# A fused attention and soft-MoE kernel rewritten: resident weights, longer q/k runs, two-bank score tiles, dispatch per batch, experts in column tiles, a hand-set order

## The chip, the core and the metric

The kernel runs on one core of a Trainium2 chip. The core has a matrix engine (TensorE, PE in the profile; its weight loads are listed apart as PEld), a vector engine (VectorE, DVE), a scalar engine (ScalarE, ACT), GpSimd (POOL) and SyncE (SP). They run side by side, each through its own list of instructions in order, and meet through semaphores. Transfers between memory and the core's buffer (SBUF) are queued by POOL or SP and carried out by 16 shared transfer engines. TensorE writes to a small accumulator memory (PSUM, eight banks of 512 float32 columns), from which VectorE and ScalarE read.

The metric is the time of one execution in microseconds, on the device. Where the profile gives a granted clock for TensorE, 1.00 stands for 2.4 GHz and 0.50 for 1.2 GHz.

## The reference, cut

Two stages follow each other. First attention with 4 batches, 8 heads, 768 positions and 64 columns per head: a head is either causal over the whole sequence or, by a flag, causal over the first 4 positions and a window of 64. Its output, 3072 tokens of 512 columns, goes through a soft mixture of 8 experts with 4 slots each.

```python
scores = scale * np.matmul(q, k.transpose(0, 1, 3, 2))
scores = np.where(mask[None], scores, -1e9)      # causal, or sinks and window, by is_retrieval[h]
a = np.exp(scores - scores.max(-1, keepdims=True))
a = a / (a.sum(-1, keepdims=True) + 1e-9)
x = np.matmul(a, v)                              # -> (3072, 512)

logits = x @ phi                                 # (3072, 32)
d = softmax(logits, axis=0)                      # over tokens
slot_input = (d.T @ x).reshape(8, 4, 512)
for e in range(8):
    slot_out[e] = np.maximum(slot_input[e] @ w1[e], 0.0) @ w2[e]   # 512 -> 1024 -> 512
c = softmax(logits, axis=1)                      # over slots
out = c @ slot_out.reshape(32, 512)
```

## The kernel before

Everything is computed in bf16 with float32 sums. The kernel is written as plain loops, and a scheduler orders the instructions of each engine by priority as buffers come free; so heads overlap.

**Setup.** POOL builds the masks, and queues the load of the eight flags (L159) ahead of the first q. VectorE makes a mask per head (L168 to L173).

**Attention** (`_attention`, a loop over 4 batches and 8 heads). For each pair of heads `_load_T2` loads q and k (L22, one transfer per head and tensor, in runs of 64 elements), transposes them on TensorE in six blocks of 128 x 128 that hold both heads (L26), and copies the result out of PSUM on VectorE (L29). v comes with one transfer per head (L50) into a tile with a column of ones; a second copy of it, v_far, is scaled by the head's flag (L56, L58) and serves key blocks more than one block away. For each of six key blocks j the scores of all later queries are computed with keys as the stationary operand (L69, 64 rows, at most 512 columns at once) into a tile of 768 float32 columns, of which there are two; ScalarE takes exp (L77), and VectorE multiplies the first 256 columns by the mask (L79). For each of six query blocks i, PV sums over j (L86, 21 matmuls of 65 columns a head), VectorE copies the sum (L90), and after all six takes the reciprocal of the ones' column (L92) and multiplies (L93) into x.

**Logits.** When attention is done, each of 24 token blocks is transposed in four pieces (L198, L199), multiplied by phi (L202), put through exp (L204) and transposed back (L206, L207). **Slots**: sums over tokens (L210 to L216), 24 matmuls of 512 columns (L223), a scaling (L225), four transposes (L228).

**Experts.** w1 and w2 of each expert, 1 MB each in bf16, are loaded by POOL (L240, L243) into rings of four buffers each. The instruction's place in POOL's list is behind all q, k and v loads. Per expert: 32 matmuls with a block of w1 as stationary operand and 4 columns (L250), relu (L256), 8 matmuls with 4 stationary columns and 512 moving columns of w2 (L259), a copy (L262) and a transfer to a scratch tensor in DRAM (L263); at the end one transfer brings all 32 rows back (L264).

**Output.** 24 matmuls of 512 columns (L270), a scaling on VectorE (L272) and a transfer by POOL that casts to float32 (L273).

## Time and profile before

| | |
|---|---|
| time, median of 3 runs (lowest to highest) | 361.65 us (361.61 to 361.93) |
| span of the profiled execution | 359.7 us |
| PE busy | 265.5 us, 74% |
| PE weight loads busy | 123.0 us, 34% |
| DVE busy | 178.2 us, 50% |
| ACT busy | 114.0 us, 32% |
| POOL busy | 113.3 us, 32% |
| moved by transfers | 32.91 MB, mean 91 GB/s |
| transfer packets, of them under 512 B | 92967, 77520 |

The profiled execution's own time is its span; the runs' median lies 1.95 us above it. The shares are averages over stages that differ: TensorE is busy nearly throughout attention and logits, and the transfer engines are busy nearly throughout the experts' stage, where the engines wait.

### The profile page before, as it was taken

How to read it: one execution, taken by the hardware profiler on the slowest of the kernel's cores; microseconds unless marked ns; L12 is line 12 of the kernel's file. 1: busy time of each engine (PE TensorE's matmuls, PEld its weight loads, DVE VectorE, ACT ScalarE, POOL GpSimd, SP SyncE). 2: the span in 40 equal slices, each digit the busy share in tenths (PEclk: the TensorE clock that was granted, in tenths of full speed). 3: DMA queues.
4: the chain of work that ended last, by engine and by line, in shares of the span. 5: the costliest groups of instructions: out<-in, count | busy, mean ns of one | idle time of the engine just before them, and what ended most of it. 6: DMA issues, size and time to landing. Idle time of an engine off the chain costs nothing.

```text
span 359.7 us, 4849 instructions
## 1 busy us (share of the span) xinstructions
PE 265.5 (74%) x1708; PEld 123.0 (34%) x1708; DVE 178.2 (50%) x725; ACT 114.0 (32%) x233; POOL 113.3 (32%) x165
## 2 busy tenths in 40 slices
PE   0048998999999999999989899996462445553661
PEld 0023444445454544545443444442221112220110
DVE  0096677676686867777576655554100000000684
ACT  1004564655646466465655211110010000000000
POOL 9395434526353453642010000006020100000463
PEclk9999999999999999999999999999876555556555
DMA  0799946959769597974230000009999999993698
GB/s 0 41 132 73 62 31 45 72 39 78 49 46 70 35 76 46 65 48 26 20 22 3 0 0 2 1 0 146 210 210 210 207 210 209 210 210 55 168 302 233
DMA packets 92967, 32.91 MB, mean 91 GB/s; under 512 B 77520, under 2 KB 85776, under 8 KB 92944
## 3 DMA queue, kind: packets, MB, share of 16 engines
q0 software_dynamic: 92832, 32.55, 74.9%
q8 instruction: 13, 0.21, 0.2%
q14 instruction: 10, 0.08, 0.1%
q1 hardware_dynamic: 112, 0.07, 0.1%
HBM read 52.53 MB, written 6.32 MB: 164 GB/s over the span
## 4 chain that ended last, share of the span: by engine, by line
PE 54%; DMA 26%; DVE 8%; POOL 5%; issue 3%; ACT 3%; POOLq 0%; DVEq 0%; SPq 0%; ACTq 0%
PE sc L69 23%; DMA w2t<-in_moe_w_dram 21%; PE pv L86 13%; PE tp L26 5%; PE tp L198 5%; PE lg L202 5%; DMA r_f__67<-in_is_retrieval_dram 4%; POOL out_dram L273 3%; ACT p_Ts L77 2%; PE sp L259 2%; DVE p_Ts L79 2%; DVE pvs L90 1%; DVE x_sb L93 1%; DVE dst L29 1%; DVE mask_j L168 1%
## 5 line engine op out<-in xcount | busy, mean ns | idle before, releaser
L77 ACT ACTIVATE p_Ts<-sc 128x768 bf16<-128x768 f32 (+2 forms) x192 | 100.3, 543 | 96.6 <-PE sc L69 91.1
L69 PE MATMUL sc<-dst 64*128 64x512 bf16 (+3 forms) x256 | 101.1, 465 | 3.8 <-ACT p_Ts L77 3.1
L86 PEld LDWEIGHTS <-p_Ts 128*128 128x128 bf16 x672 | 44.8, 127 | 51.4 <-issue 39.2
L79 DVE TENSOR_TENSOR p_Ts<-p_Ts,mask_j 128x256 bf16<-128x256 bf16 x192 | 50.2, 272 | 17.9 <-ACT p_Ts L77 15.3
L272 DVE TENSOR_SCALAR ofin<-op,rrow 128x512 bf16<-128x512 f32 x24 | 16.6, 746 | 81.9 <-PE op L270 81.3
L90 DVE COPY pvs<-pv 128x65 f32<-128x65 f32 x192 | 39.7, 222 | 33.2 <-PE pv L86 30.8
L86 PE MATMUL pv<-v_ext,p_Ts 128*128 128x65 bf16 x352 | 55.2, 244 | 1.2 <-DVE p_Ts L79 1.2
L26 PE MATMUL tp<-identity,raw 128*128 128x128 bf16 x192 | 31.5, 305 | 23.0 <-DMA raw<-in_q_dram 18.8
L259 PE MATMUL sp<-w2t,hT 128*4 128x512 bf16 x64 | 26.3, 585 | 25.6 <-DMA w2t<-in_moe_w_dram 25.6
L86 PE MATMUL pv<-v_far,p_Ts 128*128 128x65 bf16 x320 | 37.9, 243 | 3.9 <-DVE pvs L90 3.9
L22 POOL DMA_DIRECT2D raw<-in_q_dram x32 | 26.5, 834 | 35.2 <-PE pv L86 28.9
L69 PEld LDWEIGHTS <-dst 64*128 64x128 bf16 x256 | 25.4, 112 | 28.8 <-issue 14.6
L22 POOL DMA_DIRECT2D raw<-in_k_dram x32 | 26.5, 835 | 20.0 <-PE tp L26 19.6
L26 PEld LDWEIGHTS <-raw 128*128 128x128 bf16 x192 | 17.7, 131 | 35.7 <-DMA raw<-in_q_dram 22.8
L273 POOL DMA_DIRECT2D out_dram<-ofin x24 | 12.9, 536 | 50.5 <-DVE ofin L272 48.1
L240 POOL DMA_DIRECT2D w1t<-in_moe_w_dram x8 | 6.1, 767 | 71.5 <-ACT exp_lg_T L204 59.0
L50 POOL DMA_DIRECT2D v_ext<-in_v_dram x32 | 26.3, 826 | 1.8 <-issue 0.5
L199 DVE COPY xTc<-tp 128x128 bf16<-128x128 bf16 x96 | 19.5, 225 | 13.9 <-PE tp L198 12.8
L198 PE MATMUL tp<-identity,x_sb 128*128 128x128 bf16 x96 | 24.0, 282 | 1.1 <-DVE xTc L199 0.7
L202 PE MATMUL lg<-xTc,phi_sb 128*32 128x128 bf16 x96 | 23.3, 295 | 0.0
L262 ACT CAST sp_sb<-sp 4x512 bf16<-4x512 f32 x8 | 4.6, 575 | 54.9 <-PE sp L259 54.9
L259 PEld LDWEIGHTS <-hT 128*4 128x4 bf16 x64 | 7.1, 112 | 39.1 <-issue 35.2
(49 smaller groups left out, 173.5 us busy)
## 6 DMA issues: line engine op xcount, KB each, us to landing
w1t<-in_moe_w_dram POOLq DMA_DIRECT2D x8, 1024.0 KB, 34.3
w2t<-in_moe_w_dram POOLq DMA_DIRECT2D x8, 1024.0 KB, 33.5
out_dram<-ofin POOLq DMA_DIRECT2D x24, 256.0 KB, 2.3
raw<-in_q_dram POOLq DMA_DIRECT2D x32, 96.0 KB, 3.3
raw<-in_k_dram POOLq DMA_DIRECT2D x32, 96.0 KB, 3.4
v_ext<-in_v_dram POOLq DMA_DIRECT2D x32, 96.0 KB, 3.5
so_d<-sp_sb SPq DMA_DIRECT2D x8, 4.0 KB
phi_sb<-in_moe_phi_dram POOLq DMA_DIRECT2D x1, 32.0 KB, 2.9
```

What stands on the lines that cost most here:

```text
L22: nc.gpsimd.dma_start(raw[:, :, hh, :], src_ap[hh].rearrange("(so si) d -> si so d", si=P))
L26: nc.tensor.transpose(tp[:, blk * P : (blk + 1) * P], raw[:, blk, :, :].rearrange("p h d -> p (h d)"), identity)
L50: nc.gpsimd.dma_start(v_ext2[:, :, kk, :D], v[b, h + kk].rearrange("(so si) d -> si so d", si=P),)
L69: nc.tensor.matmul(sc[:, cs : cs + cl], k_T2[po : po + D, j * P : (j + 1) * P], q_T2[po : po + D, j * P + cs : j * P + cs + cl], start=Tru ...
L77: nc.scalar.activation(p_Ts[:, j, :sq_len], sc[:, :sq_len], ACT.Exp, scale=SCALE)
L79: nc.vector.tensor_mul(p_Ts[:, j, :dp], p_Ts[:, j, :dp], m[:, h, :dp])
L86: nc.tensor.matmul(pv, p_Ts[:, j, loc : loc + P], vv[:, j, :], start=(j == 0), stop=(j == i),)
L90: nc.vector.tensor_copy(pvs[:, i, :], pv)
L198: nc.tensor.transpose(tp, x_sb[:, nci, db * P : (db + 1) * P], identity)
L202: nc.tensor.matmul(lg, phi_sb[:, db, :], xTc[:, db, :], start=(db == 0), stop=(db == DB - 1))
L259: nc.tensor.matmul(sp, hT[:, fb, :], w2ts[e][:, fb, :], start=(fb == 0), stop=(fb == FB - 1))
L273: nc.gpsimd.dma_start(out[nci * P : (nci + 1) * P, :], ofin)
```

## The change

Nearly every line is new; what is computed stays. By parts:

- **Weights.** All of w1 and w2 has its own SBUF space (`w1s`, `w2s`). `w_load` queues one half of one matrix (0.52 MB in bf16, rows of 4 KB in SBUF); one is queued per pair of heads up to pair 12 and the remaining 19 at pair 13, all by POOL.
- **q and k.** One transfer per tensor and pair of heads, with six consecutive positions of 64 elements as one run per partition. The transposes then take 64 columns of one head each, 12 per tensor and pair, into rows 0 to 63 or 64 to 127 of the PSUM tile; the copy out restores the order. q is copied by VectorE, k by ScalarE.
- **Scores.** Six key blocks in three groups, (0, 4), (1, 3) and (5, 2), each in one tile of two banks (1024 columns); exp runs once per group, on 1024, 1024 and 640 columns, and the mask multiplies once per group.
- **PV** of a head stands one head behind its scores, in one PSUM tile for all six query blocks; the normalisation reads PSUM.
- **Logits, exp over tokens and dispatch** come once per batch, within attention, two to four heads after the batch has ended. phi is repeated four times over the columns, so that exp of logits fills 128 rows. The dispatch writes four groups of 32 rows, which are summed later.
- **Experts.** slot inputs are the stationary operand (32 columns), weights the moving one (512 columns); four experts write to four groups of 32 rows of one tile. A mask per expert (`emask`) keeps each one's four slots. No scratch tensor in DRAM.
- **Output.** Evictions alternate between ScalarE and VectorE into float32 tiles of three blocks; SP queues eight transfers.
- **Order.** `tc.manual_schedule()`: each engine runs its instructions as the code emits them.

The core of the diff, new lines:

```diff
+GROUPS = [[0, 4], [1, 3], [5, 2]]
+    def load_qk(self, n):
+            t = self.raw.tile([128, 2, 384], BF16, tag=tag, name=tag)
+            self.nc.gpsimd.dma_start(t, src[b, h:h + 2].rearrange("h (p s) d -> p h (s d)", s=6))
+    def transpose_qk(self, n, which):
+        for s in range(6):
+            for i in range(2):
+                self.nc.tensor.transpose(tp[64 * i:64 * (i + 1), s * 128:(s + 1) * 128],
+                                         src[:, i, s * 64:(s + 1) * 64], self.ident)
+    def qk(self, t, g):
+        sc = self.scp.tile([128, 1024], F32, tag="sc", name="sc")
+        for j in GROUPS[g]:
+            ...
+                nc.tensor.matmul(sc[:, o:o + w], kT[po:po + 64, j * 128:(j + 1) * 128],
+                                 qT[po:po + 64, q0:q0 + w], start=True, stop=True)
+        nc.scalar.activation(pT[:, GBASE[g]:GBASE[g] + GLEN[g]], sc[:, :GLEN[g]], ACT.Exp,
+                             scale=self.scale)
+    def logits(self, b):
+        for c0, cl in ((0, 512), (512, 256)):
+            for db in range(4):
+                nc.tensor.matmul(lg[:, c0:c0 + cl], self.phi4[:, db, :], self.xT[b][:, db, c0:c0 + cl],
+                                 start=(db == 0), stop=(db == 3))
+    def dispatch(self, b):
+        for i in range(6):
+            g = i % 4
+            nc.tensor.matmul(sp[32 * g:32 * (g + 1), :], self.elg[b][:, i, :], self.xb[b][:, i, :],
+                             start=(i < 4), stop=(i + 4 >= 6))
...
+    ctx.enter_context(tc.manual_schedule())
...
+        for t in range(NT + 1):
+            n = t // 2
+            if t % 2 == 0:
+                if t < NT:
+                    if n + 3 < NT // 2:
+                        at.load_qk(n + 3)
+                    if n + 2 < NT // 2:
+                        at.load_v(n + 2)
+                for _ in range(1 if n < 13 else 4 * NE):
+                    if wi < 4 * NE:
+                        w_load(wi)
+                        wi += 1
+            if t < NT:
+                at.qk(t, 0)
+                at.mask(t, 0)
+            if t >= 1:
+                at.pvmm(t - 1, 0)
+                at.pvmm(t - 1, 1)
+            if t < NT:
+                at.qk(t, 1)
+                at.mask(t, 1)
+            if t >= 1:
+                for i in (2, 3, 4):
+                    at.pvmm(t - 1, i)
+            if n + 1 < NT // 2 and t < NT:
+                at.transpose_qk(n + 1, "q" if t % 2 == 0 else "k")
+            if t < NT:
+                at.qk(t, 2)
+            if t >= 1:
+                at.pvmm(t - 1, 5)
+                at.norm(t - 1)
+            if t < NT:
+                at.mask(t, 2)
+            if t % 2 == 1 and t >= 3:
+                at.x_transpose((t - 3) // 2)
+            if t >= 8:
+                b, r = (t - 8) // 8, (t - 8) % 8
+                if r == 2:
+                    at.logits(b)
+                elif r == 3:
+                    at.exp_tokens(b)
+                elif r == 4:
+                    at.dispatch(b)
...
+            for c in range(2):
+                for do in range(4):
+                    for g in range(4):
+                        nc.tensor.matmul(hp[32 * g:32 * (g + 1), c, :], siT[:, do, :],
+                                         w1s[4 * e4 + g][:, do, c * 512:(c + 1) * 512],
+                                         start=(do == 0), stop=(do == 3))
```

How the new order stands on the engines, at three places. In each piece L-numbers are lines of the program in question.

TensorE within a head of attention. Before, the scheduler puts single transposes (`tp`, from `raw`), scores (`sc`) and PV (`pv`) between one another as they become ready:

```order
L69 LDWEIGHTS dst
L69 MATMUL sc<-dst 128x256
L69 LDWEIGHTS dst
L69 MATMUL sc<-dst 128x128
L26 LDWEIGHTS raw
L26 MATMUL tp<-identity,raw 128x128
...
L86 LDWEIGHTS p_Ts
L86 MATMUL pv<-v_ext_1752,p_Ts 128x65
L26 LDWEIGHTS raw
L26 MATMUL tp<-identity,raw 128x128
```

Now the same place, behind the PV matmuls of query block 4 and with the transposes of the next pair's q (`qr`) ahead of the last group of scores:

```order
L136 LDWEIGHTS pT
L136 MATMUL pv<-vb_134,pT 128x65
L73 LDWEIGHTS qr
L73 MATMUL tp<-ident,qr 64x128
...
L104 LDWEIGHTS kT
L104 MATMUL sc<-qT,kT 128x128
L104 LDWEIGHTS kT
L104 MATMUL sc<-qT,kT 128x384
```

The work of one kind now stands together (12 transposes in a row, then three scores), and each transpose writes 64 rows where it wrote 128.

TensorE in the experts. Before, an expert's w1 is the stationary operand and 4 columns move:

```order
L250 LDWEIGHTS w1t_3303
L250 MATMUL hp<-slot_in_T,w1t_3303 128x4
L250 LDWEIGHTS w1t_3307
L250 MATMUL hp<-slot_in_T,w1t_3307 128x4
```

Now the slots are stationary and 512 columns of w1 of four experts (`w_0` to `w_3`) move in turn, each into its own 32 rows of `hp`:

```order
L393 LDWEIGHTS siT
L393 MATMUL hp<-w_0_60,siT 32x512
L393 LDWEIGHTS siT
L393 MATMUL hp<-w_1_61,siT 32x512
L393 LDWEIGHTS siT
L393 MATMUL hp<-w_2_62,siT 32x512
L393 LDWEIGHTS siT
L393 MATMUL hp<-w_3_63,siT 32x512
```

256 matmuls of 4 columns and 64 of 512 have become 128 of 512, neighbours in different groups of rows.

POOL's list of transfers. Before, the first weights stand behind the last v load, and from the fifth expert on each load waits for a buffer:

```order
L48 MEMSET v_ext_2557 128x12
L50 DMA v_ext_2557<-in_v_dram 128x6x64 x2
L240 DMA w1t_3303<-in_moe_w_dram 128x4x1024
L243 DMA w2t_3305<-in_moe_w_dram 128x8x512
L240 DMA w1t_3307<-in_moe_w_dram 128x4x1024
```

Now one half stands behind each pair's q, k and v, and the rest behind the last v:

```order
L58 DMA qr<-in_q_dram 128x2x384
L58 DMA kr<-in_k_dram 128x2x384
L65 DMA vb_132<-in_v_dram 128x6x64 x2
L230 DMA w_6_66<-in_moe_w_dram 128x2048
L65 DMA vb_134<-in_v_dram 128x6x64 x2
L230 DMA w_6_66<-in_moe_w_dram 128x2048
L230 DMA w_7_67<-in_moe_w_dram 128x2048 x2
L235 DMA w_0_68<-in_moe_w_dram 128x2048 x2
L235 DMA w_1_69<-in_moe_w_dram 128x2048 x2
```

The weights have moved ahead of attention's end, and no load of them waits for a buffer.

## Rows read from the trace of the kernel before

**Rows 1.** Windows by stage: window, length, busy time per engine, clock, DMA share, GB/s.
```profile
core 0: us, PE busy (x) PEld busy (x) DVE busy (x) ACT busy (x) POOL busy (x), PEclk, DMA share, GB/s
25.30:200.00 174.70, 165.70 (x1103) 82.37 (x1102) 122.48 (x539) 100.28 (x192) 68.61 (x95) 1.00 0.74 48
200.00:242.40 42.40, 40.98 (x219) 18.42 (x216) 24.72 (x124) 6.41 (x24) 0.00 (x0) 1.00 0.00 1
242.40:256.20 13.80, 8.92 (x29) 3.37 (x29) 5.90 (x9) 0.00 (x0) 6.57 (x8) 1.00 0.98 162
256.20:331.20 75.00, 34.45 (x321) 14.55 (x320) 0.17 (x1) 6.04 (x16) 6.56 (x8) 0.57 1.10 195
...
334.40:359.70 25.30, 13.16 (x24) 2.55 (x24) 16.60 (x24) 0.00 (x0) 12.86 (x24) 0.50 0.90 249
```

**Rows 2.** The chain that ended last, by line, from the page.
```profile
PE sc L69 23%; DMA w2t<-in_moe_w_dram 21%; PE pv L86 13%; PE tp L26 5%; PE tp L198 5%; PE lg L202 5%; DMA r_f__67<-in_is_retrieval_dram 4%; POOL out_dram L273 3%; ACT p_Ts L77 2%; PE sp L259 2%; DVE p_Ts L79 2%; DVE pvs L90 1%; DVE x_sb L93 1%; DVE dst L29 1%; DVE mask_j L168 1%
```

**Rows 3.** Windows, four heads in the middle of attention.
```profile
103.89:125.44 21.55, 20.71 (x141) 10.52 (x142) 15.53 (x68) 12.51 (x24) 10.15 (x14) 1.00 0.88 57
```

**Rows 4.** Timeline of TensorE in attention: start us, us, engine line op, tiles.
```profile
158.20 0.61 PE L69 MATMUL sc<-dst 64*128 64x512 bf16 x1
158.74 0.34 PE L86 MATMUL pv<-v_far,p_Ts 128*128 128x65 bf16 x3
158.90 0.30 PE L86 MATMUL pv<-v_ext,p_Ts 128*128 128x65 bf16 x2
159.13 0.50 PE L69 MATMUL sc<-dst 64*128 64x384 bf16 x1
159.56 0.40 PE L86 MATMUL pv<-v_far,p_Ts 128*128 128x65 bf16 x4
```

**Rows 5.** Timeline of weight loads and matmuls around two rises of the clock.
```profile
250.87 0.15 PEld L223 LDWEIGHTS <-exp_lg 128*32 128x32 bf16 x1 [0.28 <-issue]
251.30 0.15 PEld L223 LDWEIGHTS <-exp_lg 128*32 128x32 bf16 x1 [0.28 <-issue]
251.66 1.82 PEld L223 LDWEIGHTS <-exp_lg 128*32 128x32 bf16 x9 [0.21 <-issue]
...
262.24 3.36 PE L259 MATMUL sp<-w2t,hT 128*4 128x512 bf16 x8
...
266.71 1.89 PE L259 MATMUL sp<-w2t,hT 128*4 128x512 bf16 x8 [0.74 <-DMA w2t<-in_moe_w_dram]
```

**Rows 6.** Windows, two stretches of the experts' stage.
```profile
265.00:275.00 10.00, 3.85 (x54) 2.01 (x53) 0.00 (x0) 1.44 (x4) 3.28 (x4) 0.84 1.18 209
275.00:285.00 10.00, 4.59 (x40) 1.86 (x40) 0.00 (x0) 0.77 (x2) 1.64 (x2) 0.50 1.18 209
```

**Rows 7.** Start: a piece of the chain, TensorE's first work, q's transfers from the page.
```profile
3.81 13.63 DMA r_f__67<-in_is_retrieval_dram
18.82 0.80 PE L26 MATMUL tp<-identity,raw 128*128 128x128 bf16 x6 [18.82 <-DMA raw<-in_q_dram]
raw<-in_q_dram POOLq DMA_DIRECT2D x32, 96.0 KB, 3.3
```

**Rows 8.** Groups by line and shape: busy us, mean ns, idle before.
```profile
L77 ACT ACTIVATE p_Ts<-sc 128x768 bf16<-128x768 f32 x32 | 26.0, 811 | 65.2 <-PE sc L69 61.3 <-DVE pvs L90 3.9
L77 ACT ACTIVATE p_Ts<-sc 128x128 bf16<-128x128 f32 x32 | 8.8, 276 | 4.3 <-PE sc L69 3.7
L79 DVE TENSOR_TENSOR p_Ts<-p_Ts,mask_j 128x256 bf16<-128x256 bf16 x160 | 44.4, 282 | 14.8 <-ACT p_Ts L77 12.6
L79 DVE TENSOR_TENSOR p_Ts<-p_Ts,mask_j 128x128 bf16<-128x128 bf16 x32 | 7.1, 222 | 3.1 <-ACT p_Ts L77 2.7
L29 DVE COPY dst<-tp 128x768 bf16<-128x768 bf16 x32 | 17.5, 548 | 1.1 <-PE tp L26 1.1
```

**Rows 9.** Output: an eviction's group, and windows of one stretch.
```profile
L272 DVE TENSOR_SCALAR ofin<-op,rrow 128x512 bf16<-128x512 f32 x24 | 16.6, 746 | 81.9 <-PE op L270 81.3 <-DMA out_dram<-ofin 0.6
340.00:343.00 3.00, 1.98 (x4) 0.38 (x4) 2.32 (x4) 0.00 (x0) 1.72 (x5) 0.50 1.11 309
```

More of the change, by code (lines that the diff above doesn't have):

```diff
@@ L9 @@
 from concourse._compat import with_exitstack
-from concourse.masks import make_identity
 F32 = mybir.dt.float32
@@ L266 @@
[L266 to L273 removed]
+    n_sink, window = int(n_sink), int(window)
@@ new lines, with w_load @@
+    ES = moe_phi.shape[1]
+    NE, DM, F = moe_w1.shape
+    SPE = ES // NE
+    ctx.enter_context(tc.manual_schedule())
+    singles = ctx.enter_context(tc.tile_pool(name="singles", bufs=1))
+    w1s = [singles.tile([P, 4, F], BF16, name=f"w1_{e}") for e in range(NE)]
+    w2s = [singles.tile([P, 8, DM], BF16, name=f"w2_{e}") for e in range(NE)]
+    def w_load(i):
+        if i < 2 * NE:
+            e, half = i // 2, i % 2
+            nc.gpsimd.dma_start(
+                w1s[e][:, 2 * half:2 * half + 2, :],
+                moe_w1[e].rearrange("(di do) f -> di do f", do=4)[:, 2 * half:2 * half + 2, :])
+        else:
+            e, half = (i - 2 * NE) // 2, i % 2
+            nc.gpsimd.dma_start(
+                w2s[e][:, 4 * half:4 * half + 4, :],
+                moe_w2[e].rearrange("(fi fo) d -> fi fo d", fo=8)[:, 4 * half:4 * half + 4, :])
@@ new lines @@
+    with tc.tile_pool(name="osb", bufs=4) as osb, \
+         tc.tile_pool(name="ops", bufs=6, space=PSUM) as ops:
+        for b in range(B):
+            er = expT[:, b, :].rearrange("p (t r) -> p r t", r=6)
+            ov = out[b * S:(b + 1) * S, :].rearrange("(p r) d -> p r d", r=6)
+            for half in range(2):
+                ot = osb.tile([P, 3, DM], F32, tag="ot", name="ot")
+                for r3 in range(3):
+                    r = 3 * half + r3
+                    op = ops.tile([P, DM], F32, tag="op", name="op")
+                    nc.tensor.matmul(op, er[:, r, :], slot_out, start=True, stop=True)
+                    if (6 * b + r) % 2:
+                        nc.scalar.activation(ot[:, r3, :], op, ACT.Copy, scale=rrow[:, b, r:r + 1])
+                    else:
+                        nc.vector.tensor_scalar_mul(ot[:, r3, :], op, rrow[:, b, r:r + 1])
+                nc.sync.dma_start(ov[:, 3 * half:3 * half + 3, :], ot)
```

474 lines of the change are left out of this document (262 added, 212 removed).

## The prediction

> **What bounds the kernel now.** I read the stages first [rows 1]. Each ends where its last instruction's result is wanted, and no two overlap: a start of 25.3 us before the first score matmul, 174.7 us of attention, 42.4 us of logits, 13.8 us of slots, 75.0 us of experts, 3.2 us of hand-over and 25.3 us of output. Then the chain by line [rows 2]: scores (L69) and PV (L86) hold 36% of the span, and the largest single item is the transfer of w2, 21%. So two things bound it: TensorE while attention and logits run, and the transfer queue while the experts run.
>
> In attention, four heads take 21.55 us and TensorE is busy 20.71 of them, against 15.53 for VectorE and 12.51 for ScalarE [rows 3]. A head costs 5.39 us. The column for the clock reads 1.00 there, yet the starts of matmuls say otherwise: a score of 384 columns is followed by PV 0.43 us later, one of 512 columns 0.54 us later [rows 4]. So 128 columns cost 0.11 us, 1.2 per ns, the lower of the two levels (1.2 and 2.4 GHz). The slot matmuls show the same spacing, 0.43 us, up to 251.3, and from 251.66 on nine weight loads in 1.82 us, about 0.21 us each [rows 5]; so the column's 1.00 before that moment doesn't describe the engine, and all of attention ran at 1.2 GHz. Before the rise TensorE had run the slots' full-height 512-column matmuls (L223) back to back; the experts' eight from 262.24 on are the same kind of run, and the next eight, at 266.71, go in 1.89 us [rows 5]. Some 230 us of attention and logits, TensorE busy nearly throughout, did not raise it.
>
> In the experts stage the transfers move 209 GB/s into SBUF, with the queue's share at 1.18, for 10 us on end [rows 6]; 16.8 MB of weights by that rate is 80 us, and TensorE is busy 34 of the stage's 75 us [rows 1]. The weights are not asked for before the logits end, so all of it lies in the open.
>
> **The change part by part.** I sum the new program at 1.2 GHz, stage by stage, in the profiled execution's own time; the median of the runs is 1.95 us above the span of 359.7.
>
> *Start.* Before, the first q load is queued behind the flags' load of 13.63 us, and the first transpose starts at 18.82 [rows 7]. Now the flags go through SP's queue and q is first in POOL's. Bounds for its landing: the median 3.3 us [rows 7], or again 13 us. I take 3.3, since the row with 13 us has the flag load ahead of it. With four short memsets ahead, k behind it, two sets of transposes and two copies of 0.55 us [rows 8], the first score matmul comes at 8 us (7 to 16).
>
> *A head in attention.* Scores: 2688 columns as before, 2.24 us at 0.43 per 512. PV: 21 matmuls, 0.054 apart (three between 158.74 and 158.90), 1.13 us. Transposes: they double from 6 to 12 per head, since each takes one head's 64 columns; two neighbours write the two halves of the array's columns. If they run together, six times 128 columns at 1.2 per ns, 0.64 us; one by one 1.27. Changes between 64-row scores and full-height work cost: 512 columns are 0.43 us by the spacing of the slot matmuls [rows 5], and 0.54 where PV follows; the second of the two PV from 158.90, so at 158.95, is followed by scores after 0.18 instead of 0.05 [rows 4]; about 0.12 each. The new order has seven per head, 0.84 us; before there are 302 over 32 heads by the program's order, 9.4 each, 1.13 us. What is left of the 5.39 after 2.24, 1.13, 0.64 and 1.13 is 0.25 us of waits; I take 0.30. Sum: 5.15 us a head (5.78 with single transposes), 165 us for 32.
>
> *ScalarE and VectorE* I cost at nothing under that cover. Exp of 1024, 1024 and 640 columns by the line through 768 and 128 columns [rows 8] is 1.03 + 1.03 + 0.70; half a copy of k, 0.41 at most, and logits' share 0.1 give 3.26 us a head. VectorE: three masks of 512, 512 and 384 columns, 0.40 + 0.40 + 0.34, normalising 384 columns under the 0.55 of a copy of 768, a reciprocal under the 0.22 of a mask of 128, half of two copies 0.55, far values of 260 columns 0.28: 2.74 us. Both are below 5.15. If TensorE doubles its speed, ScalarE's 3.26 is the bound; that is the second rival.
>
> *Logits and slots* move into attention: transposes of x, 15 × 0.64 = 9.6 us; per batch 3072 columns of logits 2.56, six transposes 0.64, six one-column sums 0.3 at PV's spacing, dispatch of six 512-column matmuls in four column tiles 0.85 (two rounds), two changes 0.24: 4.6 us, three times 13.8. The fourth is in the tail. So attention is 165 + 9.6 + 13.8 = 188 us. The long full-height runs may raise the clock for a while; between 265 and 275 it was up for part of the time (0.84) and from 275 on no more [rows 6], so a rise lasts some 7 us and saves 3. For two of three batches I take 6 us off: 182.
>
> *Tail to the experts.* Last PV 1.1, normalising 0.8, transposes of x and copy 1.2, logits 2.56, exp 0.8, transposes and copy 0.9, dispatch 0.85, add and scaling 0.75 each like an eviction [rows 9], slot transposes and copy 0.6: 10.3, with hand-overs 11 us. It replaces 42.4 + 13.8.
>
> *Experts.* 128 matmuls of 512 columns, four at a time in column tiles: 32 rounds. The first 16 at 0.43, 6.8 us; relu 0.6; 16 transposes 1.7 and a copy 0.9; the second 16 between 3.5 us at 0.21 and 6.8, I take 5.2; copies 0.4. 16 us instead of 75, and the round trip through DRAM (3.2) is gone.
>
> The Trainium skill, page "TensorE: Matmul & The Clock Gate", Part 3, says that a weight load overlaps a running matmul only where the two use different rows of the array; column tiles share all rows, so by it each of the four would wait for its neighbour. The trace does not agree: loads of the same rows lie inside the 0.43 us of the running 512-column matmul and cost nothing [rows 5]. By the page the sum would be that of the first rival, by the row it stays.
>
> *Weights.* 32 halves of 0.52 MB. POOL queues one per pair of heads, and from pair 13 on the last 19 without any wait; the wait ahead of them is for pair 11's buffer, some 24 heads in, at 8 + 24 × 5.47 + 9 = 148 us (5.47 with the share of x's transposes, 9 for two batches' logits and slots). 19 × 0.52 MB at 209 GB/s is 48 us, so they land by 196; the second half of the experts, which wants them, starts at 8 + 182 + 11 + 8 = 209. Attention hides them, with 13 us to spare. Ahead of that POOL has two q/k loads fewer per pair. Twelve loads keep the queue at 0.88 for 21.55 us [rows 3]; a pair now brings four loads and 2.5 us of weights in 10.9 us.
>
> *Output.* 6.3 MB at the 309 GB/s that a full stretch shows [rows 9] is 20.4 us; ahead of it three matmuls and an eviction of 0.75, 2 us. Twelve evictions on each of two engines, 9 us, lie beneath. 22 us (18 to 25), before 25.3.
>
> Sum: 8 + 182 + 11 + 16 + 22 = 239, plus 2 outside the span: **241 us**. With the start, the spells and the output at their ends, 228 to 258.
>
> **Rivals.**
>
> *Column tiles run one after another.* No row of before has neighbours in different column tiles, so nothing here shows that they share the array. Then transposes add 0.63 × 32 = 20 us, dispatch 4 × 1.7 = 7, and the experts need 14 matmuls at 0.43 and 114 at 0.21, 30.5 us instead of 12, 18.5 more: 241 + 46 = **287 us**. For it: the doubled transposes would be a plain loss. Against: the loads at least are free [rows 5]. The Trainium skill's page "TensorEngine Tiling (Array Packing)", Key Properties, says that different tiles load and multiply in parallel; no run here shows it yet.
>
> *The clock rises in attention and stays.* The logits put 2.56 us of full-height work on TensorE without a gap, next to PV and dense scores, from head 10 on. If that raises the clock and ScalarE's waits don't lower it, 11 heads take 60 us, a first batch 3, and the other 21 take ScalarE's 3.26, say 3.4 us: 8 + 60 + 3 + 71 = 142. The weights now bound: queued at about 8 + 60 + 3 + 13.5 × 3.4 = 117, landed at 165, then 0.5 + 0.4 + 22 + 2: **190 us**. Against: the rises of before ended when TensorE had little to do [rows 5, 6], and at 3.4 us a head it has gaps. A clock that comes and goes gives times between 190 and 235. The Trainium skill, page "TensorE: Matmul & The Clock Gate", Part 1, says that activity releases the throttle and idleness restores it; attention at 1.2 GHz with TensorE busy 20.71 of 21.55 us [rows 3] shows that being busy alone is not enough.
>
> *Slower: the score tiles serialise the head.* With two tiles of two banks, TensorE might have to wait for exp and mask of each group, in an order that nothing can rearrange. Then a head costs 5.15 + 2.76 + 1.14 = 9.05 us, 32 of them 290, in all 290 + 23 + 8 + 11 + 16 + 22 + 2 = **372 us**. It decides from (361.65 - 241)/32 = 3.8 us of waiting per head. Against: each group's exp has one other group and a run of PV to hide behind, and before, with the same number of tiles, waits are 0.3 us.
>
> *The weights are not there in time.* If the burst of 19 goes at two thirds of 209 GB/s beside other loads, it lands at 220 instead of 196, and the experts wait some 11 us: 252. It belongs to the forecast's upper end.
>
> **How the numbers follow.** Forecast, 1.2 GHz with column tiles side by side: 0.45. Clock up for good or for long: 0.30 (0.2 near 190, 0.1 between). Tiles in turn: 0.20. Serial: 0.02. Between 258 and 275 through several small waits: 0.03. The likeliest is 241. Eight in ten: below 186 I leave 0.05, above 275 some 0.15; the range is 186 to 275, and the forecast's own 228 to 258. Faster by over 0.2%, about what can be told from no change here: 0.97; within it 0.01; slower 0.02.
>
> **What would show it.** First score matmul at 8 us. A head every 5.2 to 5.5 us with TensorE above 90% busy; starts of transposes in pairs; PV 0.054 apart (0.027 if the clock is up). Experts' matmuls starting in fours. Nothing waiting for weights. Output at 300 GB/s or more. I am wrong if scores of 512 columns start 0.21 us apart through attention, if neighbours in column tiles start 0.43 apart, or if TensorE waits for exp or weights.

## The result

The changed kernel takes 206.44 us (median of four runs, 203.79 to 216.89) where the kernel before takes 361.65; the ratio is 0.565 [0.5634, 0.5667]. That ratio is taken from the two fast runs (203.79 and 204.94); in the other two TensorE's mean granted clock was lower, 0.83 and 0.78 against 0.89 and 0.85. The forecast of 241 was 35 us too high. What came is the second rival in its milder form, a clock that comes and goes, between 190 and 235, which the prediction gave a chance of 0.1.

The profiled execution took 203.79 us, 202.0 of it in the span. Its windows by stage, the answer to [rows 1]: start, attention up to batch 0's logits, these with their dispatch, the stretch behind them, the rest of attention, the tail, the experts, the output.

```profile
core 0: us, PE busy (x) PEld busy (x) DVE busy (x) ACT busy (x) POOL busy (x), PEclk, DMA share, GB/s
0.00:8.44 8.44, 1.71 (x25) 1.23 (x25) 3.62 (x10) 2.08 (x2) 7.32 (x20) 1.00 0.77 75
8.44:64.30 55.86, 54.15 (x465) 29.77 (x466) 38.07 (x104) 33.13 (x38) 27.66 (x44) 1.00 1.10 133
64.30:79.00 14.70, 13.26 (x145) 7.62 (x145) 8.12 (x22) 8.42 (x12) 3.78 (x6) 0.88 0.82 111
79.00:104.00 25.00, 22.63 (x319) 14.09 (x318) 19.41 (x51) 20.64 (x26) 13.19 (x18) 1.00 1.14 140
104.00:155.90 51.90, 48.59 (x568) 28.32 (x566) 34.69 (x88) 36.11 (x43) 18.59 (x31) 0.80 1.08 171
155.90:163.40 7.50, 3.59 (x35) 2.02 (x36) 3.44 (x10) 0.90 (x2) 1.06 (x2) 0.93 1.06 212
163.40:182.14 18.74, 12.74 (x145) 5.38 (x145) 2.52 (x4) 2.76 (x4) 0.00 (x0) 0.77 0.76 152
182.14:202.00 19.86, 7.97 (x23) 3.12 (x23) 8.73 (x12) 7.92 (x12) 0.00 (x0) 0.67 0.76 317
```

Attention with three batches' logits is now 147.5 us. The second line and the fourth both show 1.00 in the clock's column, but 55.86 us hold 465 matmuls and 25.00 us hold 319. The first 1.00 stands before the clock's first record, as in [rows 4]; the spacing tells the level. The timeline of TensorE (start us, us, engine line op, tiles) ahead of the first rise, across it, and in the fast stretch:

```profile
33.46 1.03 PE L104 MATMUL sc<-qT,kT 64*128 64x512 bf16 x3
34.42 0.34 PE L136 MATMUL pv<-vb,pT 128*128 128x65 bf16 x3
...
64.34 0.62 PE L166 MATMUL lg<-xT,phi 128*128 128x512 bf16 x1
65.17 1.82 PE L166 MATMUL lg<-xT,phi 128*128 128x512 bf16 x6 [0.22 <-issue]
66.92 0.60 PE L104 MATMUL sc<-qT,kT 64*128 64x512 bf16 x3
...
83.33 0.60 PE L104 MATMUL sc<-qT,kT 64*128 64x512 bf16 x3
83.87 0.27 PE L136 MATMUL pv<-vb,pT 128*128 128x65 bf16 x3
84.07 0.60 PE L104 MATMUL sc<-qT,kT 64*128 64x512 bf16 x3
```

Batch 0's logits start at 64.34 and still run at 1.2 GHz: from 65.17 to 66.92 they stream two times 512 and four times 256 columns, 2048 columns in 1.75 us. Right behind them the clock is up (its first record is a rise at 66.8 us): the three scores from 66.92 take 0.60 us where the same three took 1.03 at 33.46. In the fast stretch 1024 columns of scores from 83.33 have PV following after 0.54 us, where it was 0.96 at 33.46. Two windows, each of two pairs of heads without logits, one at either level:

```profile
29.92:50.58 20.66, 20.66 (x181) 11.51 (x182) 14.39 (x38) 12.40 (x15) 7.13 (x11) 1.00 1.10 151
79.59:93.16 13.57, 12.47 (x181) 7.63 (x180) 11.49 (x29) 11.98 (x15) 7.26 (x10) 1.00 1.12 130
```

The same work takes 10.33 us a pair with TensorE busy for all of it, or 6.8 us with ScalarE busy for 88% and TensorE waiting. So each pair at the higher level saves 3.5 us. That ScalarE sets the pace there is read from its share alone.

The chain by line, the answer to [rows 2]:

```profile
DMA w<-in_moe_w_dram 25%; PE sc L104 18%; PE pv L136 12%; PE tp L73 6%; ACT pT L110 5%; DMA out_dram<-ot 3%; POOL vb L65 2%; PE tpx L157 2%; PE op L432 2%; PE lg L166 2%; DVE pT L126 2%; DVE qT L79 1%; DVE xb L147 1%; POOL qr L58 1%; POOL kr L58 1%
```

TensorE's timeline in the experts:

```profile
163.45 6.44 PE L393 MATMUL hp<-w,siT 128*32 128x512 bf16 x64 [0.38 <-DVE siT L386]
169.82 0.71 PE L405 MATMUL tph<-ident,hs 128*128 128x128 bf16 x8
...
172.11 2.12 PE L416 MATMUL sp<-w,hT 128*32 128x512 bf16 x35
176.90 1.05 PE L416 MATMUL sp<-w,hT 128*32 128x512 bf16 x16 [2.67 <-DMA w<-in_moe_w_dram]
179.36 1.86 PE L416 MATMUL sp<-w,hT 128*32 128x512 bf16 x13 [1.41 <-DMA w<-in_moe_w_dram]
```

The first half of the experts takes 6.4 us. The second half waits twice for its weights; they are the largest item of the chain again, 25%, though most of them now load beside attention.

### The profile page after: what moved, and what is told of

It reads as the page before. It is cut to its first block, busy times and chain, and to the rows that moved or that the text cites. A ratio compares the mean times of both kernels' runs of the same rounds, so it can differ in the third digit from the quotient of the medians.

```text
span 202.0 us, 4145 instructions
## 1 busy us (share of the span) xinstructions
PE 164.6 (82%) x1711; PEld 91.6 (45%) x1716; DVE 118.6 (59%) x296; ACT 112.0 (55%) x137; POOL 71.6 (35%) x118
## 4 chain that ended last, share of the span: by engine, by line
PE 44%; DMA 28%; ACT 7%; POOL 7%; DVE 6%; issue 4%; ACTq 0%; POOLq 0%
DMA w<-in_moe_w_dram 25%; PE sc L104 18%; PE pv L136 12%; PE tp L73 6%; ACT pT L110 5%; DMA out_dram<-ot 3%; POOL vb L65 2%; PE tpx L157 2%; PE op L432 2%; PE lg L166 2%; DVE pT L126 2%; DVE qT L79 1%; DVE xb L147 1%; POOL qr L58 1%; POOL kr L58 1%
## 5 line engine op out<-in xcount | busy, mean ns | idle before, releaser
L110 ACT ACTIVATE pT<-sc 128x1024 bf16<-128x1024 f32 (+1 forms) x96 | 86.0, 918 | 38.1 <-PE sc L104 35.9
L104 PE MATMUL sc<-qT,kT 64*128 64x128 bf16 (+3 forms) x288 | 68.7, 360 | 1.8 <-DVE msk L295 0.9
L126 DVE TENSOR_TENSOR pT<-pT,msk 128x512 bf16<-128x512 bf16 (+1 forms) x96 | 38.0, 401 | 30.2 <-ACT pT L110 29.7
L136 PEld LDWEIGHTS <-pT 128*128 128x128 bf16 x672 | 32.3, 111 | 33.4 <-issue 21.6
L136 PE MATMUL pv<-vb,pT 128*128 128x65 bf16 x352 | 39.5, 216 | 4.6 <-DVE pT L126 4.5
L104 PEld LDWEIGHTS <-kT 64*128 64x128 bf16 x288 | 21.9, 106 | 26.6 <-issue 15.0
L136 PE MATMUL pv<-vf,pT 128*128 128x65 bf16 x320 | 30.9, 218 | 0.0
L65 POOL DMA_DIRECT2D vb<-in_v_dram x32 | 26.8, 843 | 0.9 <-DVE xb L147 0.7
L147 DVE TENSOR_TENSOR xb<-pv,rs 128x384 bf16<-128x384 f32 x32 | 17.8, 557 | 1.1
L235 POOL DMA_DIRECT2D w<-in_moe_w_dram x16 | 8.5, 536 | 25.0 <-DMA w<-in_moe_w_dram 24.6
L79 DVE COPY qT<-tp 128x768 bf16<-128x768 bf16 x16 | 15.3, 954 | 0.6
## 6 DMA issues: line engine op xcount, KB each, us to landing
qr<-in_q_dram POOLq DMA_DIRECT2D x16, 192.0 KB, 5.8
kr<-in_k_dram POOLq DMA_DIRECT2D x16, 192.0 KB, 4.5
```

The source lines that it names most:

```text
L65: self.nc.gpsimd.dma_start(vb[:, i, :, :64], self.v[b, h + i].rearrange("(so si) d -> si so d", si=128))
L79: self.nc.vector.tensor_copy(o, i)
L104: nc.tensor.matmul(sc[:, o:o + w], kT[po:po + 64, j * 128:(j + 1) * 128], qT[po:po + 64, q0:q0 + w], start=True, stop=True)
L110: nc.scalar.activation(pT[:, GBASE[g]:GBASE[g] + GLEN[g]], sc[:, :GLEN[g]], ACT.Exp, scale=self.scale)
L126: nc.vector.tensor_mul(v, v, m)
L136: self.nc.tensor.matmul(pv[:, i, :], pT[:, o:o + 128], vv[:, hh, j, :], start=(j == 0), stop=(j == i))
```

## The experiments

I had three things to settle: what raised the clock and whether that is where the 35 us went; whether the column tiles really run side by side; and which row misled me at the two ends of the program. Ratios are to the kernel before, with the interval.

**1. No logits inside attention.** The block of the loop that calls logits, exp_tokens and dispatch is removed, and behind attention stands:

```diff
-        at.logits(B - 1)
-        at.exp_tokens(B - 1)
-        at.dispatch(B - 1)
+        for b in range(B):
+            at.xT[b], at.xb[b] = at.xT[B - 1], at.xb[B - 1]
+            at.logits(b)
+            at.exp_tokens(b)
+            at.dispatch(b)
```

> Logits, exp and dispatch of the first three batches leave attention and run behind it, each of the four on the last batch's x (so the slots of the other batches are not those of the reference; the work has the same shapes). Theory, that the full-height logits and dispatch inside attention raise TensorE's clock: no rise in the clock's record before attention ends, a pair of heads takes 10.3 us all through, attention ends at 8.4 + 32 x 5.17 = 174, tail 11 and three batches of 3 to 4.6 us more give 195 to 199, experts 13 (weights are there by 196, so no waiting), output 20, 2 outside: 228 to 238 us. Rival, that attention raises its clock by itself or that the time saved came from elsewhere: pairs of heads at 6.8 us still stand in attention, and the total stays at 204 to 217.

Measured: 227.81 us, 0.629 [0.628, 0.631]; three runs lie between 227.27 and 228.22, a fourth took 365.78, and what happened in it no kept trace shows. Windows of eight pairs of its attention and of the tail with four batches:

```profile
58.00:140.66 82.66, 82.66 (x722) 46.09 (x722) 46.73 (x112) 49.60 (x56) 32.69 (x47) 1.00 0.92 111
173.12:193.96 20.84, 13.57 (x119) 7.15 (x117) 6.80 (x19) 3.60 (x8) 0.00 (x0) 0.95 0.72 145
```

The clock's row of its page, 40 slices of the span:

```profile
PEclk9999999999999999999999999999999999599985
```

Eight pairs in 82.66 us are 10.33 each, TensorE busy in every one of them, and the last PV stands at 173.12 instead of 155.7. The first record of the clock, a rise at 178.4 us, comes only behind the start of the late logits (174.9). So the first rise moves with the logits, and attention by itself did not raise the clock in these 165 us. The experts no longer wait for weights.

The logits are not the only thing that can raise it, though. In the kernel of run 5 below, whose attention is the changed kernel's line for line, the clock's first record is a rise at 39.25 us, 16 us ahead of the first logits (55.67). Two pairs of heads without logits in that trace:

```profile
40.84:54.63 13.79, 12.54 (x183) 7.67 (x180) 11.52 (x31) 11.96 (x15) 6.72 (x10) 1.00 1.17 144
```

They take 6.9 us each. In the changed kernel itself the rises at 114.6 and 148.7 us come 5.6 us or more behind the end of the last dispatch, with heads in between. Why attention alone raised the clock in these places and not in 165 us of run 1 no trace shows.

**2. A clock raised at the start.**

```diff
+        nc.vector.memset(expT[:, 0, :512], 0.0)
...
+        junk = at.scp.tile([P, 1024], F32, tag="sc", name="junk")
+        for i in range(10):
+            nc.tensor.matmul(junk[:, :512], expT[:, 0, :P], expT[:, 0, :512], start=True, stop=True)
         at.transpose_qk(0, "q")
```

> Ten full-height matmuls of 512 columns of zeros into a score tile, before the first q is there (about 1 to 5 us), as extra work whose result nobody reads. Theory: the clock rises at the start, before the first head, and the first heads cost 3.4 instead of 5.17 us for as long as attention keeps it up; up to batch 0's logits that is 10 heads x 1.77 = 18 us at most. If all of that comes, attention ends near 138, but the last weights were the end's bound already, and they move only with pair 11's buffer: about 188 to 196. Rival 1, attention alone doesn't hold the clock: it falls again within two heads, 200 to 206. Rival 2, the dummies delay the first transposes by up to 1.5 us and nothing else: 205 to 208.

Measured: 207.14 us (204.99 to 208.61), 0.568 [0.566, 0.570], no gain. The timeline of the start:

```profile
1.26 4.29 PE L302 MATMUL junk<-expT 128*128 128x512 bf16 x10 [1.26 <-DVE expT L269]
5.48 0.53 PE L73 MATMUL tp<-ident,qr 128*64 128x128 bf16 x12
6.82 0.53 PE L73 MATMUL tp<-ident,kr 128*64 128x128 bf16 x12 [0.82 <-DMA kr<-in_k_dram]
8.24 0.39 PE L104 MATMUL sc<-qT,kT 64*128 64x512 bf16 x1 [0.90 <-ACT kT L82]
```

A window of the first 50 us of attention:

```profile
8.24:57.98 49.74, 47.31 (x410) 26.10 (x411) 34.32 (x95) 29.38 (x33) 24.41 (x39) 0.50 1.12 137
```

The dummies did raise the clock: the twelve transposes at 5.48 take 0.53 us where they took 0.85 without. The rise is gone when the heads begin: it ends at 8.7 us, and the window from the first score on shows 0.50. But TensorE stood idle for 0.82 and 0.90 us between the dummies and the first score, so the run does not tell whether attention would have held the clock; in the changed kernel it did for up to 27 us. The time lies in rival 2's range, the early fall is rival 1's sign. The next rise, at 59.9 us, again comes ahead of the first logits (62.5).

**3. Two weight halves per pair.**

```diff
-                for _ in range(1 if n < 13 else 4 * NE):
+                for _ in range(2):
```

> Two weight halves per pair of heads from the first pair on, so 32 are queued by pair 15 and the burst of 19 at pair 13 is gone. Theory, that the last weights' landing bounds the end: the two waits of the slot-out matmuls for DMA (2.7 and 1.4 us, with the wait behind them some 5 us) vanish, and the time is 199 to 202 at the same share of the clock. Rival, that the queue is the real bound: two halves (4.9 us of queue) beside a pair's q, k, v (about 5.5 us) fill 10.4 us, more than a pair of heads at the higher clock takes (6.8), so q, k or v come late in the fast stretches, and the time is 204 to 215.

Measured: 210.32 us median, 202.08 to 213.13; too uneven to give a verdict against the changed kernel. In the profiled run the waits for weights are gone as the theory said: the second half runs in one piece:

```profile
183.44 3.64 PE L416 MATMUL sp<-w,hT 128*32 128x512 bf16 x64
```

But two windows show attention slower, and a third, of two pairs of heads further on, shows it fast:

```profile
64.30:79.00 14.70, 13.69 (x130) 6.76 (x127) 7.86 (x22) 8.34 (x11) 4.35 (x7) 0.85 1.14 171
79.00:107.60 28.60, 28.60 (x261) 16.43 (x261) 16.25 (x39) 17.02 (x20) 11.86 (x17) 0.50 1.11 152
127.58:141.19 13.61, 12.55 (x185) 7.68 (x182) 10.85 (x28) 11.97 (x15) 8.40 (x13) 1.00 1.29 177
```

In the second TensorE is busy all the 28.60 us, and in the third a pair takes 6.8 us as in the changed kernel, so q, k and v did not come late, and the rival falls too. The clock was down in a stretch in which it was up before (the fourth line of the stages above): this time it did not rise again at the first dispatch. While the clock goes up and down like this, it moves the time by more than the weights do.

**4. Neighbours in the same column tile.** The loop over g goes outside the loop over do.

> In the experts' first half the loop over the four column tiles goes outside the loop over the four slices of the contraction, so that neighbours lie in the same column tile; same matmuls, other order. Theory, that neighbours in different column tiles run side by side: the 64 matmuls take 64 x 0.213 = 13.6 us at the higher clock or up to 27 at the lower, instead of 6.4; the second half then finds its weights there, so the total grows by 2 to 16 us. Rival, that column tiles give nothing and the 6.4 us is the higher clock's work hidden otherwise: 6.4 us again, total unchanged.

Measured: 202.66 us in the one run. The timeline:

```profile
167.61 6.17 PE L393 MATMUL hp<-w,siT 128*32 128x512 bf16 x64 [0.38 <-DVE siT L386]
```

6.17 us for the 64: my expectation failed, and the rival's number came. In both kernels most of these matmuls stand at 1.2 GHz. Either tiles give nothing, or order does not matter. The next run tells these apart.

**5. One column tile for all.**

```diff
-                        nc.tensor.matmul(hp[32 * g:32 * (g + 1), c, :], siT[:, do, :],
+                        nc.tensor.matmul(hp[0:32, c, :], siT[:, do, :],
...
-                                         start=(do == 0), stop=(do == 3))
+                                         start=(do == 0 and g == 0), stop=(do == 3 and g == 3))
```

> The 64 matmuls of the experts' first half all go into the first column tile (the four experts of a set are summed into the same 32 partitions, the other partitions are zero, so slots and output are not those of the reference); number, shape and order of the matmuls are the same. Before the run with the order changed the 64 took 6.2 us though neighbours lay four by four in one tile, so order alone doesn't separate the tiles. Theory, that tiles run side by side and order doesn't matter because each tile takes its next matmul when it is free: one tile alone needs 64 x 0.213 = 13.6 us at the higher level or up to 27 at the lower. Rival, that 32-column matmuls are simply cheaper than I thought: 6.2 us again.

Measured: 211.90 us in the one run. The timeline:

```profile
164.98 9.01 PE L394 MATMUL hp<-w,siT 128*32 128x512 bf16 x32 [1.51 <-DVE hp L390]
176.73 7.07 PE L394 MATMUL hp<-w,siT 128*32 128x512 bf16 x32 [2.73 <-DVE hp L390]
```

The same 64 matmuls take 9.01 + 7.07 = 16.1 us in one tile (the waits ahead are for the zeroing that this kernel adds), 6.2 to 6.4 us in four. So tiles run side by side, and, with the run before, that holds also where the code has four neighbours in one tile.

**6. Full-height scores.** k of one head stands in a tile whose other 64 rows are zero (the lines that make and clear the tiles are left out here):

```diff
-                nc.tensor.matmul(sc[:, o:o + w], kT[po:po + 64, j * 128:(j + 1) * 128],
-                                 qT[po:po + 64, q0:q0 + w], start=True, stop=True)
+                nc.tensor.matmul(sc[:, o:o + w], kT[hh][:, j * 128:(j + 1) * 128],
+                                 qT[:, q0:q0 + w], start=True, stop=True)
...
-            self.nc.scalar.copy(o, i)
+            self.nc.scalar.copy(self.kz[n % 2][0].rearrange("c (p s) -> c p s", s=6)[:64], i[:64])
+            self.nc.vector.tensor_copy(self.kz[n % 2][1].rearrange("c (p s) -> c p s", s=6)[64:], i[64:])
```

> Scores over all 128 rows: k transposed of one head stands in a tile whose other 64 rows are zero, q of both heads streams past it; the copy of k out of PSUM becomes two copies of 64 rows, one by ScalarE, one by VectorE. Columns, exps, masks and results are the same; no change between 64-row and 128-row work is left, and all of attention is full-height. Theory 1, that the 64-row scores keep TensorE's clock low: the clock rises in the first pairs and stays up, a pair takes ScalarE's 6.8 us nearly everywhere, attention ends near 125 to 135, and the weights (19 halves at 2.45 us after pair 11's last PV, near 100) land near 150: 172 to 182. Theory 2, that the clock goes its way as before and only the seven changes of 0.12 us per head vanish: a cold pair takes 10.33 - 1.7 = 8.6 us, rises come after the logits of each batch only, 190 to 200. Rival, that changes cost nothing and the clock is as before: pairs of 10.33, 203 to 217.

Measured: 193.2 us (192.0 to 196.7), 0.532 [0.531, 0.533]. The clock's row:

```profile
PEclk9999999699999999999979999996999969958965
```

A window of attention with batch 0's dispatch and batch 1's logits in it:

```profile
60.00:95.00 35.00, 25.63 (x390) 18.67 (x392) 28.40 (x68) 24.58 (x31) 15.96 (x23) 1.00 1.09 133
```

The timeline where scores and PV follow each other, to be read against 83.33 to 84.07 above:

```profile
100.05 0.61 PE L109 MATMUL sc<-qT,kz 128*128 128x512 bf16 x3
100.49 0.26 PE L141 MATMUL pv<-vb,pT 128*128 128x65 bf16 x3
100.59 0.60 PE L109 MATMUL sc<-qT,kz 128*128 128x512 bf16 x3
```

The first record, a rise, is at 20.31 us, long before any logits (54.8), and the clock stays up in attention but for spells of a few us. The three other traces with full-height scores (runs 7 and 8) have their first record at 17.6 to 17.9 us; of the nine with 64-row scores none shows a rise within attention before 39.25. That is theory 1 for the clock, with one thing open: the edit takes out the half height and the changes between 64-row and 128-row work together, and no run tells which of the two kept the clock down. The time is not theory 1's 172 to 182, as two things of the expectation did not come. A pair takes 7.55 us instead of 6.8, with VectorE busiest (28.40 of 35.00). And the experts again wait 5.0 us for weights. The changes between 64 and 128 rows are priced by the way, at the higher level: scores of 1024 columns to PV 0.44 us instead of 0.54, three PV to scores 0.10 instead of 0.20.

**7. Full-height scores with two halves per pair**, the edits of 6 and 3.

> Full-height scores together with two weight halves per pair. With full-height scores alone attention ended at 145.0, the experts' first half began at 152.8 and the second at 160.3, and it waited 5.0 us for weights that landed only at 169. Theory, that there the weights are the end's bound: the second half takes 3.3 us and ends near 163.6, output 20, 2 outside: 186 (183 to 190) instead of 193.2, with no wait for weights. Rival, that two halves beside q, k and v overfill the queue now that a pair takes 7.6 us: q or k come late in attention, and the time is 192 or more.

Measured: 187.35 us (186.92 to 188.31), 0.518 [0.516, 0.521]. The timeline of the experts' second half:

```profile
160.59 3.64 PE L421 MATMUL sp<-w,hT 128*32 128x512 bf16 x64
```

A window of two pairs of heads:

```profile
66.00:82.00 16.00, 12.51 (x191) 9.04 (x189) 14.06 (x34) 12.66 (x15) 7.42 (x12) 1.00 1.34 200
```

Now that the clock holds, the edit that could not be told in run 3 is worth 6 us: the second half runs in one piece of 3.64 us.

**8. Both copies of k on ScalarE**, on top of run 7, in two runs.

> As the kernel with full-height scores and two halves per pair, but both 64-row copies of k are ScalarE's. Theory, that at the higher clock VectorE's chain holds a pair at 7.55 us (its copy of 64 x 768 costs 0.96, and with only the one copy on ScalarE a pair at the higher clock took 6.8): pairs of 7.0, 13 of them, so about 6 us less: 178 to 184. Rival, that ScalarE becomes the bound with 0.79 us more per pair: pairs of 7.6 to 8, 186 to 192.

> The kernel with full-height scores, two halves per pair and both copies of k on ScalarE once more, since the profiled run of the first time had a granted clock of 0.56 where the others had 1.0 and its pairs can't be read. Theory, VectorE's chain held a pair at 7.55: pairs of 7.0 at the higher clock and 184 (182 to 187). Rival, ScalarE is the bound now: pairs of 7.6 to 8 at the higher clock and 187 or more.

Measured: 186.55 us (184.00 to 208.45), 0.512 [0.508, 0.516], and 186.22 us (185.48 to 187.02), 0.515 [0.514, 0.516]. This is the lowest median, 0.6% under run 7's, with intervals that meet. The profiled execution of the first, 208.45 us, had a granted clock of 0.56 where the second's has 1.00, so the window, of two pairs, is from the second:

```profile
68.00:84.00 16.00, 11.99 (x197) 8.74 (x192) 11.89 (x30) 14.38 (x18) 8.37 (x12) 1.00 1.34 200
```

VectorE falls from 14.06 to 11.89 us of 16, ScalarE rises from 12.66 to 14.38, and a pair takes 7.50 instead of 7.55. The theory had 7.0, the rival 7.6 to 8; ScalarE is the busiest engine now, 90%, as the rival had it.

**9. The ends of the program.** First the output through POOL's queue, cast on the way; then the flags on POOL's queue; then both ends in forms of the kernel before (shown in part; the flags' tile becomes float32, and what reads it follows):

```diff
-        nc.sync.dma_start(ri, bass.AP(tensor=ir32, offset=0, ap=[[0, P], [1, 2 * H]]))
+        nc.gpsimd.dma_start(ri, bass.AP(tensor=ir32, offset=0, ap=[[0, P], [2, H], [1, 1]]))
...
-                nc.sync.dma_start(ov[:, 3 * half:3 * half + 3, :], ot)
+                    nc.sync.dma_start(ov[:, r, :], ot[:, r3, :])
```

> Output as before: the eviction writes BF16 and POOL's queue casts to F32 on the way to DRAM, instead of F32 tiles by SP's queue. Theory, that the 6.3 MB move at 309 GB/s this way and at some 424 the other: from the first output matmul to the end 22 to 25 us instead of 19.9, total up by 2 to 5 us at the same share of the clock. Rival, that the stage is bound by the 24 evictions: no change.

> The flags' load goes back to POOL's queue, ahead of the first q. Theory, that this load is what held the start of the kernel before: first q transpose near 18 instead of 4.9 us, first score near 21 instead of 8.4, total up by 10 to 13 us, less what the later start lets the weights catch up. Rival, that the load was slow for another reason: first score at 8 to 10, total 204 to 217.

> Both ends of the changed kernel in the forms of the kernel before, each read from its own stage. Start: the flags as 1024 single 4-byte elements, cast on the way, by POOL's queue ahead of the first q. With the 64-byte rows on POOL's queue the first transpose came at 5.96, so the queue alone was not it. Theory, that the form of the load held the start: first transpose near 18, first score near 21. Rival: 5 to 7 again, then the start of the kernel before was held by its q loads. Output: 24 pieces of 256 KB with runs of 2 KB by SP's queue instead of 8 of 768 KB with runs of 6 KB. Theory, that the length of the runs sets the rate: slices near 309 GB/s, the stage 22 us instead of 19.9. Rival, that the eviction pace did: slices near 420, the stage 19 to 20.

TensorE's first work in the changed kernel:

```profile
4.86 0.85 PE L73 MATMUL tp<-ident,qr 128*64 128x128 bf16 x12 [4.86 <-DMA qr<-in_q_dram]
```

With the flags' load on POOL's queue:

```profile
5.96 0.85 PE L73 MATMUL tp<-ident,qr 128*64 128x128 bf16 x12 [5.96 <-DMA qr<-in_q_dram]
```

With the load on that queue and in the form of before:

```profile
17.32 0.85 PE L73 MATMUL tp<-ident,qr 128*64 128x128 bf16 x12 [17.32 <-DMA qr<-in_q_dram]
```

That load among the page's transfers (KB each, us to landing):

```profile
ri<-in_is_retrieval_dram POOLq DMA_DIRECT2D x1, 4.0 KB, 15.0
```

The queue alone costs 1.1 us, not the 13 of the theory; the 1024 single elements, cast on the way, 11.4 more. Elements and cast were not told apart. A window of ten microseconds in the output, first the changed kernel's:

```profile
185.00:195.00 10.00, 5.33 (x18) 2.08 (x16) 6.70 (x10) 6.44 (x10) 0.00 (x0) 0.84 0.99 413
```

By POOL's queue with the cast:

```profile
208.00:218.00 10.00, 2.09 (x6) 0.62 (x5) 3.76 (x6) 3.33 (x6) 2.14 (x4) 0.63 1.16 425
```

In runs of 2 KB by SP's queue:

```profile
196.00:206.00 10.00, 3.11 (x10) 1.11 (x9) 5.07 (x8) 4.42 (x7) 0.00 (x0) 0.78 1.03 382
```

From the first output matmul to the end it takes 22.05 us by POOL's queue and 20.0 in runs of 2 KB, 19.86 with neither. The first of these lies in its theory's 22 to 25, but not for the theory's reason: the cast and POOL's queue leave the rate where it was, and 1.6 of the 2.2 us lie behind the last byte (the transfers end 3.6 us ahead of the span's end, in the changed kernel 2.0). Runs of 2 KB cost less than a tenth of the rate. Neither gives the 309 GB/s of [rows 9], so both theories fall. What is left is the pace of before: one engine's evictions, busy 2.32 of those 3.00 us. That was not tried. The totals of these three runs (225.3, 219.1, 214.4 us) differ from 203.8 by more than the ends. In the first two the clock was down for longer in attention: the last PV stands at 179.5 and 177.3 us instead of 155.7. In the third it stands at 170.3, and the start accounts for 11.6 us of that (first score at 20.0 instead of 8.44).

## Why the prediction was right and wrong

The measured column is the profiled execution's, 203.79 us in all.

| term, us | predicted | measured |
|---|---|---|
| start | 8 | 8.44 |
| attention with three batches' logits | 182 | 147.5 |
| tail | 11 | 7.5 |
| experts | 16 | 18.7 |
| output | 22 | 19.9 |
| outside the span | 2 | 1.8 |

Attention is 34.5 us too high, and the other terms' errors nearly cancel (2.7 us the other way). The wide range, 186 to 275, held because of the chances given to the rivals; the forecast's own, 228 to 258, did not. Its lower end does not follow from the terms either: the start at 7 and the output at 18 take 241 down to 236, and no low end of the spells is stated that gives 228.

**The step that failed** is the credit for the clock, "For two of three batches I take 6 us off". Attention without logits, all at 1.2 GHz, is 173.12 - 8.11 = 165.0 us in run 1. With the prediction's 13.8 for three batches it would have been 178.8; it was 147.5, so the clock gave back 31 us instead of 6, which is 25 of the 34.5. The credit came from the rises of [rows 6], which ended when TensorE had little to do in the experts. I carried their length over to attention, where TensorE has work again at once: a rise there lasted up to 27 us (77.0 to 104.3). The right effect stood in the prediction as the second rival, with its price (3.4 us a head; 6.8 a pair measured) and its bound (ScalarE, 88% busy); I gave it 0.30, 0.1 of that for the milder form that came, and the cold case 0.45.

**A head at 1.2 GHz** was costed at 5.15, and 5.47 with x's transposes; run 1 gives 10.33 / 2 = 5.17 for the latter. The difference is the term "I take 0.30" for waits, which is zero: TensorE is busy 82.66 of 82.66 us. 32 times 0.30 is 9.6, all of what attention at 1.2 GHz was off (165 + 9.6 = 174.6 against 165.0).

**Column tiles side by side** held, in the six dispatch matmuls, the transposes (twelve in 0.78 us at the lower level, 74.34 to 75.12, a change included) and the experts (6.4 us, predicted 6.8). Run 5 shows what the first rival would have cost, 16.1 us for half the experts' work. The Trainium skill, page "TensorEngine Tiling (Array Packing)", Key Properties, says that different tiles load and multiply in parallel; the traces agree (64 in 6.4 us against 16.1 in one tile). The Trainium skill, page "TensorE: Matmul & The Clock Gate", Part 3, lists a weight load as overlapping only a matmul of other rows, though the same Part also has loads to a background weight buffer pulled ahead. Here loads for all 128 rows stand inside the 0.43 us of the running matmuls, and the measurement decides; the prediction's "By the page the sum would be that of the first rival" took the first sentence alone. One such group of loads in the changed kernel:

```profile
163.86 0.16 PEld L393 LDWEIGHTS <-siT 128*32 128x32 bf16 x4 [0.27 <-issue]
```

**The weights** were to land at 196 and be wanted at 209. They landed at 179.4 and were wanted at 172.1, and the two waits for them, 4.1 us, are why the experts took 18.7 us. The rate was right, 213 GB/s; the burst does not go "without any wait", POOL waits 24.6 us in all for earlier weights while it queues the last of them, but the transfers keep to 210 to 216 GB/s meanwhile. The margin was worked out for the cold case alone. The faster clock pulled the demand forward by 37 us and the landing, which starts at pair 11's buffer and then runs at the queue's pace, by 17. The rival with the clock up said it, "The weights now bound".

**The tail** ran at the higher level, which the sum did not count on: batch 3's logits span 1.6 us instead of 2.56. **The start** is right in number and only half in reason: the flags' load was the cause, but by its 1024 single elements with their cast, not by standing in POOL's queue (run 9). **The output** was sized from a row in which, it seems, something else set the pace; the transfers can do 413 GB/s. **ScalarE and VectorE** were hidden as said in the cold stretches. Two of their terms: exp of 1024 columns measures 1.02 (taken 1.03); VectorE's copy of q, which writes a permuted order, 0.95 against the 0.55 of [rows 8], an under-sized term that mattered only at the higher clock. The serial rival did not come: no wait in the cold stretch.

What stays open: what ends a rise, and what besides the logits starts one. In the changed kernel the clock rose again at 77.0, during the first dispatch (from 76.2); in run 3 it did not during the same one, from 75.8; the traces don't show why. The times of the changed kernel's four runs go with the clock: 203.8 us at a mean granted clock of 0.89, 216.9 at 0.78.

## What to carry to other kernels

Read TensorE's level from the spacing of matmuls before pricing a stage, and price the stage at both levels; where the two are 30 us apart, the question of what raises the clock is the prediction. Here TensorE, busy throughout with half-height matmuls mixed with narrow ones, stayed at 1.2 GHz for 165 us in one run (in another it rose at 39 us); padding the other 64 rows with zeros, which adds no columns, had it up within the first heads and made 206 us into 193. When one term moves the demand for a transfer, work out its landing again for that case: the same burst of weights had 13 us to spare in the one case and was 7 us late in the other.

## What the runs showed of the hardware

Matmuls in four column tiles overlap even when the code puts four of one tile in a row: 6.17 us for 64, as in alternating order (6.44). The Trainium skill, page "TensorE: Matmul & The Clock Gate", Part 3, says that matmuls start and end strictly in the order of the program. Run 4 speaks against it: its matmuls start in fours, and one tile alone takes 0.22 us for each (32 in 7.07 us in run 5). The first four:

```profile
167.61 0.65 PE L393 MATMUL hp<-w,siT 128*32 128x512 bf16 x4 [0.38 <-DVE siT L386]
```

This holds if the compiled list keeps the order of the code; the trace doesn't name the tile of a matmul.

A change between 64-row scores and 128-row work costs 0.10 us at the higher level, and 0.11 at the lower: there PV follows 1024 columns of scores after 0.96 us, and 1024 columns by themselves are 0.85 at 1.2 per ns. A load of 1024 elements of 4 bytes took 15.0 us to land, one of 128 rows of 64 bytes, without a cast, 2.8 on the same queue.
